# Attention interleaved with an MoE layer: six attention bursts in a group become five, two bursts of group 0 move, and the loads of batches 2 and 3 are asked for later

## Chip, cores and metric

One Trainium2 chip, one core of it. The time is the device time of one execution in microseconds (us). The engines are named as in the profile: PE (TensorE matmul), PEld (its weight loads), DVE (VectorE), ACT (ScalarE), POOL (GpSimd) and SP (SyncE, which here only issues DMAs).

## What is computed

Eight batches of attention (8 heads, 576 positions, 64 dimensions) feed a two-layer MoE block over 8 x 576 = 4608 tokens. The reference, cut to what matters:

```python
q_d, k_d, v_d = (t.reshape(B, H, 144, 4, 64).mean(axis=3) for t in (q, k, v))
out_d     = softmax(q_d @ k_d.T / 8) @ v_d                 # on means of 4 positions
out_up    = np.repeat(out_d, 4, axis=2)
out_local = softmax(where(|i - j| < 4, q @ k.T / 8, -1e9)) @ v
x = (out_up + out_local).transpose(0, 2, 1, 3).reshape(4608, 512)
h = x @ w_in                                               # 512 -> 2048
y = (h / (1 + exp(-1.702 * h))) @ w_out                    # 2048 -> 512
```

## The kernel before

**Groups.** The MoE block runs in nine groups `g` of 512 tokens. `mm1` makes 16 blocks of hidden features (`ffc`), four matmuls of 128x512 each (L706), and ACT turns each block into `gT` (L717). `mm2` multiplies `gT` with `w_out` in 64 matmuls (L771), and `store` evicts each 128 tokens through ACT (`osb`, L756) and asks SP for the output DMA (L761).

**Steps.** The attention of batch `b = g + 1` is cut into steps and laid between the MoE matmuls of group `g` at fixed positions: 0 to 15 are the blocks of `mm1`, and from 16 on one position is one matmul of `mm2`. The order on every engine is the program's order (a manual schedule); engines meet through semaphores that the tile framework sets. The positions are lists:

```python
POS = [13, 16, 33, 44, 55, 65, 74]
POS_0 = [16, 18, 27, 48, 52, 57, 66, 70, 75]
VDP_0 = 44
```

`POS` serves groups 1 to 6 (batches 2 to 7), `POS_0` and `VDP_0` serve group 0 (batch 1). Batch 0 comes ahead of group 0 with code of its own. Groups 7 and 8 hold no attention. A step that puts work on PE is called a burst here. For `POS` the steps are: scores of the first four heads (13), their exponentials on ACT (16, no PE work), scores and exponentials of the other four (33), `avn(0, 1)` (44) and `avn(2, 3)` (55), which multiply the exponentials with the values for two head pairs each, and `tr(0, 1)` (65) and `tr(2, 3)` (74), which turn two head pairs each. That is six bursts. In group 0 the turns come one head pair at a time, and `VDP_0` is one more burst: `prep_vd_pe(1)` (L335) makes the mean values of batch 1 on PE out of `vbs[1]`, which ten DMAs of `load_vb` fill.

**One head pair `hp`.** `av` writes its output to a PSUM tile; `normalise` (DVE: a reciprocal at L477, a product at L478) makes `y`; `transp` (PE: L502 and L487) writes the turned `x` to a PSUM tile; `copy_od` (ACT, two copies, L617) widens the downsampled part into `od`; `merge` (DVE: L638 and a small L644) adds both into `xT[hp]`, the operand of the next group's `mm1`. `xT[hp]` is the hp-th of the four contraction blocks. For groups above 1, `mm1` starts with six matmuls on blocks 0 to 2 and takes block 3 after them.

**PSUM.** Three tiles `PA[0..2]` go round (`ps_tile`), two small ones `PM` serve the MoE blocks. In group 0 the AV outputs and turned tiles use `PA[1]` and `PA[2]` by name.

**Loads.** POOL issues the loads that change the type: `load_qk` (L199; k and q of four heads as bf16, four DMAs for a batch), `load_vb` (L230), `load_w_in`, `load_w_out` (L261). SP issues `load_v` (L219, ten DMAs into the single tile `vf`), `load_v4` (L242, six DMAs) and the stores. In group 0 POOL issues the q/k loads of batch 2 right behind the last `w_out` load, and then a one-element copy (L807) from `w_out` into `vf`, which holds SP's `load_v(2)` until that `w_out` part has landed. In group 1 `load_v(3)` is issued as soon as `prep_v(2)` has read `vf`.

**Preparation in a group.** DVE transposes k and q (`prep_qk`, L276); POOL then, in this order, averages k of the first heads (`pool_qk`, L294 and L297), issues the next batch's q/k loads, casts the values (`prep_v`, L308), averages q, then k and q of the other heads, and last the values (`prep_v4`, L314 and L317). `avn(0, 1)` needs the end of this chain.

Of the kernel before, what the change touches and what calls it, by code (L numbers as in the profile page):

```python
# [8 lines left out]
FP32 = mybir.dt.float32  # L9
# [10 lines left out]
def kernel(  # L20
# [171 lines left out]

    qf, kf, vf = {}, {}, {}

    def load_1(name, src, store, b, qd):
        t = ldp.tile(
            [128, 1152], BF16, name=f"{name}b{qd}", tag=f"{name}b{qd}", bufs=2
        )
        nc.gpsimd.dma_start(  # L199
            out=t,  # L200
            in_=bass.AP(
                tensor=src.tensor, offset=src[b, 4 * qd].offset,
                ap=[[1152, 128], [1, 1152]],
            ),
        )
        store[b, qd] = t

    def load_qk(b, qd):
        load_1("k", k, kf, b, qd)
        load_1("q", q, qf, b, qd)  # L210

    def load_v(b, gate=None, chunks=range(5)):
# [93 lines left out]
    def prep_v(b, eng, i=slice(0, 5), h=slice(0, H)):  # L306
        cp = eng.copy if eng is nc.scalar else eng.tensor_copy
        cp(out=vbs[b % 2][:, i, h, 0:D], in_=vf[b][:, i, h])  # L308
# [14 lines left out]
    def flat(p):  # L323
        return p.rearrange("p x n -> p (x n)")
# [298 lines left out]
    def sub(t, off, *dims):  # L623
        return bass.AP(
            tensor=t.tensor, offset=t.offset + off,
            ap=[list(t.ap[0])] + [list(d) for d in dims],
        )
# [3 lines left out]
    def merge(b, hp, x, od, eng=None):  # L631
        t0 = b * S
        eng = eng or nc.vector
        if eng is nc.gpsimd:
            xs = work.tile([128, 2, 512], BF16, name="xs", tag="xs", bufs=2)
            nc.scalar.copy(out=xs[:, :, 0:288], in_=x[:, :, 0:288])
            x = xs
        eng.tensor_tensor(  # L638
            out=sub(xT[hp], t0 + 3, (57, 2), (114, 5), (1, 57)),
            in0=sub(x, 3, (509, 2), (57, 5), (1, 57)),  # L640
            in1=sub(od, 3, (57, 2), (114, 5), (1, 57)),
            op=ALU.add,
        )
        eng.tensor_tensor(  # L644
            out=sub(xT[hp], t0, (573, 2), (1, 3)),
            in0=sub(x, 0, (512 + 285, 2), (1, 3)),
            in1=sub(od, 0, (573, 2), (1, 3)),
            op=ALU.add,
        )
# [12 lines left out]
    def attention(b, slots=None):  # L662
        st = {}

        def s_pe(qd):
            if qd == 0:
                st["s", qd], st["d", qd] = scores_mixed(b, qd)
            else:
                st["s", qd] = scores(b, qd)
                st["d", qd] = scores_d(b, qd)  # L670

        def s_act(qd):
            if qd == 0:
                nc.scalar.preload_act_table_set("exp_and_others")
            exp_local(qd, st["s", qd])
            exp_down(qd, st["d", qd])
            if qd == 1:
                nc.scalar.preload_act_table_set("silu_and_others")
            mask_local(qd)

        def s1():
            s_pe(1)
            s_act(1)

        def avn(*hps):
            def f():
                ns = [slots and slots[hp % 2] for hp in hps]
                for hp, o in zip(hps, av(b, hps, ns)):
                    st["y", hp] = normalise(o)
            return f  # L690

        def tr(*hps):
            def f():
                ns = [slots and slots[hp % 2] for hp in hps]
                for hp, x in zip(hps, transp(hps, [st["y", hp] for hp in hps], ns)):
                    od = copy_od(hp, x)
                    merge(b, hp, x, od)
            return f

        first = [lambda: s_pe(0), lambda: s_act(0), s1, avn(0, 1)]  # L700
        if b == 1:
            return first + [tr(0), tr(1), avn(2, 3), tr(2), tr(3)]
        return first + [avn(2, 3), tr(0, 1), tr(2, 3)]

    def hps_mm(g, ffc, dmc, acc):
        nc.tensor.matmul(  # L706
# [32 lines left out]
    def mm2(g, gT, steps):  # L739
        tok0 = g * TG  # L740
        n = 0

        if g == 0:
            order = [(t0 + u, 4 * c + f)
                     for t0, c in ((0, 0), (0, 1), (2, 0), (2, 1),
                                   (0, 2), (2, 2), (0, 3), (2, 3))
                     for u in range(2) for f in range(4)]
        else:
            order = [(t, ffc) for t in range(4) for ffc in range(n_ffc)]
        ops = {}  # L750

        def store(t, ap, c0, n, eng, q):
            r0 = tok0 + 128 * t
            osb = moe_sb.tile([128, n], FP32, name="osb", tag=f"osb{n}", bufs=4 if n == 512 else 3)
            if eng is nc.scalar:
                eng.activation(out=osb, in_=ap, func=AF.Copy, scale=1.0 / GELU_SCALE)  # L756
            else:
                eng.tensor_single_scalar(  # L758
                    out=osb, in_=ap, scalar=1.0 / GELU_SCALE, op=ALU.mult
                )  # L760
            q.dma_start(out=out[r0 : r0 + 128, c0 : c0 + n], in_=osb)  # L761

        for t, ffc in order:
            if g == n_groups - 1 and t == 3:
                continue
            for f in steps.get(n, ()):
                f()
            n += 1
            if ffc == 0:
                ops[t] = PA[0][:, t - 2, :] if g == 0 and t > 1 else pm_tile()  # L770
            nc.tensor.matmul(  # L771
                ops[t],
                lhsT=gT[:, ffc, t * 128 : (t + 1) * 128],
                rhs=w_out_bf[:, ffc, :],
                start=(ffc == 0), stop=(ffc == n_ffc - 1),
            )
            if ffc == n_ffc - 1 and not (g == 0 and t == 2):
                for u in (2, 3) if g == 0 and t == 3 else (t,):
                    store(u, ops[u], 0, d_model, nc.scalar, nc.sync)

        if g == n_groups - 1:
            for h in range(2):
                cols = slice(256 * h, 256 * h + 256)
                p = pm_tile()
                for ffc in range(n_ffc):
                    nc.tensor.matmul(  # L786
                        p[:, 0:256],
                        lhsT=gT[:, ffc, 384:512],
                        rhs=w_out_bf[:, ffc, cols],
                        start=(ffc == 0), stop=(ffc == n_ffc - 1),  # L790
                    )
                if h == 0:
                    store(3, p[:, 0:256], 0, 256, nc.scalar, nc.sync)
                else:
                    store(3, p[:, 0:128], 256, 128, nc.scalar, nc.scalar)
                    store(3, p[:, 128:256], 384, 128, nc.vector, nc.sync)
        for f in steps.get(n, ()):
            f()

    POS = [13, 16, 33, 44, 55, 65, 74]  # L800
    POS_0 = [16, 18, 27, 48, 52, 57, 66, 70, 75]
    VDP_0 = 44

    o, y, x = {}, {}, {}

# [93 lines left out]
    for g in range(n_groups):  # L899
        b = g + 1  # L900
        if g == 0:
            nc.gpsimd.memset(v4[32:64], 0.0)
            load_vb(1, 0)
            load_vb(1, 1)
            prep_qk(1, 0)
            pool_qk(1, 0)
            load_vb(1, 2)
            prep_qk(1, 1)
            pool_1(1, 1, "q", nc.vector)
            pool_qk(1, 1, "k")  # L910
            load_vb(1, 3)
            load_vb(1, 4)
            load_w_out(2)
            load_w_out(3)
            for qd in range(NQ):
                load_qk(2, qd)
            load_v(2, gate=after(w_out_bf[0:1, 12, 0:1], nc.gpsimd))
            load_v4(2)
        elif b < B:
            if b > 2:  # L920
                load_v4(b)
            prep_qk(b, 0)
            pool_qk(b, 0, "k")
            if b + 1 < B:
                for qd in range(NQ):
                    load_qk(b + 1, qd)
            prep_v(b, nc.gpsimd)
            if b + 1 < B:
                load_v(b + 1)
            pool_qk(b, 0, "q")  # L930
            prep_qk(b, 1)
            pool_qk(b, 1)
            prep_v4(b, nc.gpsimd)
        steps = {}
        if b < B:
            for n, f in zip(POS if g else POS_0, attention(b, None if g else (1, 2))):
                steps.setdefault(n, []).append(f)
            if g == 0:
                steps.setdefault(VDP_0, []).append(lambda: prep_vd_pe(1, flat(PA[2])))
        gT = new_gT() if g else gT0  # L940
        mm1(g, gT, steps, 0 if g else 6)
        mm2(g, gT, {n - 16: f for n, f in steps.items() if n >= 16})
# [30 lines left out]
```

The softmax here doesn't subtract the row's maximum and nothing guards it: scores larger than these inputs give would overflow.

## Time and profile before

| | |
|---|---|
| runs | 320.34, 324.53, 326.18, 320.25 us |
| median | 322.43 us |
| profiled execution: time, and span in the trace | 320.34 us, 318.6 us |
| PE busy | 311.5 us (98%) |
| ACT, POOL, DVE busy | 183.0, 140.9, 135.3 us |
| granted TensorE clock | 1.000 |
| group 0 from its first step to its end | 38.09 to 60.11 us |
| a group with attention (group 3) | 33.21 us |
| a group without attention (group 7) | 27.72 us |
| DMA moved | 40.02 MB |

The span runs from the first to the last instruction of the program; the time has 1.7 us around it. PE is busy nearly all the time, so a group's length is read from the PE rows, and the other engines matter where PE waits for them. Starts are in us from the beginning of the span. A timeline row gives start, length, engine, line, operation, output and inputs, shapes and count, and in brackets the idle time before it and what ended it.

### The profile page before, as it was taken

The page shows a single profiled execution, that of the slowest core. Times are in us where ns is not written, and L with a number is a line of the kernel's source. Part 1 is how long each engine was busy: PE and PEld are TensorE (multiplying, and loading weights), DVE is VectorE, ACT ScalarE, POOL GpSimd, SP SyncE. Part 2 cuts the span into 40 slices and gives each one's busy share as a digit, 9 for nine tenths or more (in the row PEclk, how much of TensorE's full clock was granted, in tenths as well). Part 3 has the DMA queues.
Part 4 walks back from the last instruction along what each step waited for, and adds up shares of the span by engine and source line. Part 5 has one row for each costly group of instructions (what it writes and reads, how often), then busy time and mean ns, then how long its engine had stood idle before and what let it go on. Part 6 is the DMA issues. An engine that isn't in the chain of part 4 may idle for free.

```text
span 318.6 us, 10869 instructions
## 1 busy us (share of the span) xinstructions
PE 311.5 (98%) x4860; PEld 156.9 (49%) x4860; DVE 135.3 (42%) x224; ACT 183.0 (57%) x317; POOL 140.9 (44%) x172
## 2 busy tenths in 40 slices
PE   7899999999999999999999999999999999999995
PEld 3664554445544555455545544555455544444444
DVE  6983626812674077605670478046811650000000
ACT  4555772667457664668365936593667367315611
POOL 8993960299109930794069604980296000000000
PEclk9999999999999999999999999999999999999999
DMA  7999999899619931994179615981450110020011
GB/s 121 116 196 210 183 140 214 170 200 264 171 61 200 218 96 63 210 207 117 69 165 220 149 70 128 210 194 37 126 92 3 70 68 0 5 95 33 0 67 67
DMA packets 63550, 40.02 MB, mean 126 GB/s; under 512 B 44048, under 2 KB 54416, under 8 KB 63504
## 3 DMA queue, kind: packets, MB, share of 16 engines
q0 software_dynamic: 18864, 14.95, 32.9%
q1 hardware_dynamic: 44496, 24.32, 32.0%
q8 instruction: 38, 0.62, 0.8%
q14 instruction: 8, 0.07, 0.1%
q10 hardware_dynamic: 144, 0.07, 0.1%
HBM read 44.83 MB, written 9.44 MB: 170 GB/s over the span
## 4 chain that ended last, share of the span: by engine, by line
PE 92%; DMA 4%; DVE 1%; POOL 1%; issue 1%; ACT 0%; POOLq 0%; DVEq 0%
PE pm L771 36%; PE pm L706 34%; PE pa L706 6%; PE pa L375 3%; PE pa L771 2%; DMA qb<-in_q_dram 2%; PE pa L394 2%; PE pa L461 2%; PE pa L502 2%; DMA vb<-in_v_dram 1%; PE pa L446 1%; PE pm L786 1%; PE pa L487 1%; DVE y L478 1%; PE pa L590 1%
## 5 line engine op out<-in xcount | busy, mean ns | idle before, releaser
L771 PE MATMUL pm<-w_out_bf,gT 128*128 128x512 bf16 x528 | 121.8, 380 | 0.0
L706 PE MATMUL pm<-xT,w_in_bf 128*128 128x512 bf16 x488 | 109.7, 379 | 0.0
L717 ACT ACTIVATE gT<-pm 128x512 bf16<-128x512 f32 x122 | 72.7, 598 | 38.3 <-PE pm L706 38.2
L706 PEld LDWEIGHTS <-w_in_bf 128*128 128x128 bf16 x576 | 55.6, 98 | 67.1 <-issue 1.9
L771 PEld LDWEIGHTS <-gT 128*128 128x128 bf16 x560 | 51.6, 98 | 59.2 <-issue 0.5
L425 DVE TENSOR_TENSOR es<-es,mask 128x600 bf16<-128x600 bf16 x28 | 20.2, 742 | 82.0 <-ACT es L411 81.6
L294 POOL TENSOR_TENSOR pq<-kT 128x576 f32<-128x576 bf16 x14 | 16.1, 1148 | 85.9 <-DVE kT L276 85.8
L756 ACT ACTIVATE osb<-pm 128x512 f32<-128x512 f32 (+2 forms) x35 | 20.5, 586 | 56.6 <-PE pm L771 52.9
L478 DVE TENSOR_TENSOR y<-pa,rc 128x896 bf16<-128x896 f32 x28 | 30.6, 1091 | 1.0
L638 DVE TENSOR_TENSOR xT<-pa,od 128x570 bf16<-128x570 f32 x28 | 21.1, 753 | 11.8 <-ACT od L617 11.8
L617 ACT COPY od<-pa 128x384 f32<-128x384 f32 (+1 forms) x56 | 18.5, 411 | 12.6 <-DVE xT L644 7.7
L314 POOL TENSOR_TENSOR v<-v 112x512 f32<-112x512 f32 x18 | 24.0, 1331 | 0.0
L758 DVE TENSOR_SCALAR osb<-pm 128x128 f32<-128x128 f32 x1 | 0.3, 292 | 54.8 <-ACT osb L756 54.8
L276 DVE STREAM_TRANSPOSE kT<-kb 128x576 f32<-128x576 f32 x16 | 20.0, 1248 | 3.3 <-DMA kb<-in_k_dram 3.1
L411 ACT ACTIVATE es<-pa 128x600 bf16<-128x600 f32 x32 | 19.7, 667 | 2.7 <-PE pa L375 2.3
L706 PE MATMUL pa<-xT,w_in_bf 128*128 128x512 bf16 x88 | 21.1, 379 | 0.0
L276 DVE STREAM_TRANSPOSE qT<-qb 128x576 f32<-128x576 f32 x16 | 19.9, 1241 | 0.4
L717 ACT ACTIVATE gT<-pa 128x512 bf16<-128x512 f32 x22 | 12.1, 603 | 8.5 <-PE pa L706 8.4
L230 POOL DMA_DIRECT2D vb<-in_v_dram x20 | 13.7, 700 | 6.2 <-DMA w_in_bf<-in_moe_w_in_dram 4.1
L375 PE MATMUL pa<-qT,kT 32*64 32x60 bf16 x1280 | 15.5, 201 | 1.0 <-DVE qT L276 1.0
L375 PEld LDWEIGHTS <-kT 32*64 32x64 bf16 x1280 | 13.8, 103 | 4.5 <-DVE es L425 3.0
L417 ACT ACTIVATE ed<-pa 128x864 bf16<-128x864 f32 x16 | 14.3, 896 | 2.0 <-PE pa L394 1.8
(98 smaller groups left out, 281.2 us busy)
## 6 DMA issues: line engine op xcount, KB each, us to landing
out_dram<-osb SPq DMA_DIRECT2D x35, 256.0 KB, 2.1
vf<-in_v_dram SPq DMA_DIRECT2D x60, 128.0 KB, 4.7
v<-in_v_dram SPq DMA_DIRECT2D x36, 192.0 KB, 5.0
kb<-in_k_dram POOLq DMA_DIRECT2D x16, 288.0 KB, 8.3
qb<-in_q_dram POOLq DMA_DIRECT2D x16, 288.0 KB, 9.4
w_out_bf<-in_moe_w_out_dram POOLq DMA_DIRECT2D x4, 512.0 KB, 8.9
vb<-in_v_dram POOLq DMA_DIRECT2D x20, 64.0 KB, 5.5
w_in_bf<-in_moe_w_in_dram POOLq DMA_DIRECT2D x2, 512.0 KB, 6.2
```

Of the source, the lines that this page charges most:

```text
L276: nc.vector.transpose(out=t32.rearrange("p (i c) -> p c i", c=18), in_=store[b, qd].bitcast(FP32).rearrange("p (c d) -> p c d", c=18),)
L314: eng.tensor_tensor(out=t1[0:112], in0=x[:, :, 0:2, :], in1=x[:, :, 2:4, :], op=ALU.add)
L375: nc.tensor.matmul(sp[r // 2][64 * par : 64 * par + 64, r % 2, 60 * i : 60 * i + 60], lhsT=kT[b, qd][rows, k0 : k0 + 64, a], rhs=qT[b, qd] ...
L411: nc.scalar.activation(out=es[2 * qd + u][:, :, 0:300], in_=sp[u][:, :, 0:300], func=AF.Exp, scale=inv_sqrt_d,)
L425: nc.vector.tensor_tensor(out=ev, in0=ev, in1=mask, op=ALU.mult)
L478: nc.vector.tensor_tensor(out=y[:, xs], in0=ov[:, :, :, 0:D], in1=rc[:, xs].to_broadcast([128, n, 7, D]), op=ALU.mult,)
L617: nc.scalar.copy(out=od[:, 4 * t0 : 4 * (t0 + n)].rearrange("p (t f) -> p t f", f=4), in_=x[:, xx, 288 : 288 + n, None].to_broadcast([128, ...
L638: eng.tensor_tensor(out=sub(xT[hp], t0 + 3, (57, 2), (114, 5), (1, 57)), in0=sub(x, 3, (509, 2), (57, 5), (1, 57)), in1=sub(od, 3, (57, 2) ...
L706: nc.tensor.matmul(acc, lhsT=w_in_bf[:, dmc, ffc * 128 : (ffc + 1) * 128], rhs=xT[dmc][:, g * TG : g * TG + TG], start=(dmc == 0), stop=(d ...
L717: nc.scalar.activation(out=gT[:, ffc, :], in_=acc, func=AF.Silu, scale=GELU_SCALE)
L756: eng.activation(out=osb, in_=ap, func=AF.Copy, scale=1.0 / GELU_SCALE)
L771: nc.tensor.matmul(ops[t], lhsT=gT[:, ffc, t * 128 : (t + 1) * 128], rhs=w_out_bf[:, ffc, :], start=(ffc == 0), stop=(ffc == n_ffc - 1),)
```

## The change

- **Five bursts.** For batches 2 to 7 `avn(2, 3)` and the turn of head pair 0 become one step, `av_and_turn`, at 57; the turns of head pairs 1, 2 and 3 become one step at 70. `merge` of head pair 0 goes from DVE to POOL there: [...]ACT copies the local part of `x` to `xs` in SBUF first. `xs` becomes narrower (288 columns instead of 512) with one buffer.
- **Group 0.** The steps of batch 1 move: the mean values from 44 to 36, `avn(0, 1)` from 48 to 40, the turns of head pairs 0 and 1 from 52 and 57 to 47 and 53, `avn(2, 3)` from 66 to 63. The turns of head pairs 2 and 3 stay at 70 and 75.
- **q and k of batch 2** are no longer asked for ahead of `load_v(2)`. POOL issues them behind the turn of head pair 2, and a one-element copy from `y` of head pair 2 (the third AV output) into the k tile holds them until that `y` is there.
- **v of batch 3** is asked for by SP at position 65 of group 1, behind the store of position 64, instead of behind `prep_v(2)`.
- **Order on POOL.** In groups 1 and 2 POOL averages q of the first heads ahead of `prep_v`.
- The small `osb` tiles get two buffers instead of three.

```diff
-    def load_qk(b, qd):
-        load_1("k", k, kf, b, qd)
+    def load_qk(b, qd, gate=None):
+        load_1("k", k, kf, b, qd, gate)          # load_1 calls gate(t[0:1, 0:1]) ahead of its DMA
         load_1("q", q, qf, b, qd)
...
+        w = 512
         if eng is nc.gpsimd:
-            xs = work.tile([128, 2, 512], BF16, name="xs", tag="xs", bufs=2)
-            nc.scalar.copy(out=xs[:, :, 0:288], in_=x[:, :, 0:288])
-            x = xs
+            xs = work.tile([128, 2, 288], BF16, name="xs", tag="xs", bufs=1)
+            nc.scalar.copy(out=xs, in_=x[:, :, 0:288])
+            x, w = xs, 288
...
         if b == 1:
-            return first + [tr(0), tr(1), avn(2, 3), tr(2), tr(3)]
-        return first + [avn(2, 3), tr(0, 1), tr(2, 3)]
+            def next_qk():
+                tr(2)()
+                load_qk(2, 0, after(st["y", 2][0:1, 0, 0, 0:1], nc.gpsimd))
+                load_qk(2, 1)
+
+            return first + [tr(0), tr(1), avn(2, 3), next_qk, tr(3)]
+
+        def av_and_turn():
+            os = av(b, (2, 3), (None, None))
+            x, = transp([0], [st["y", 0]], [None])
+            for hp, o in zip((2, 3), os):
+                st["y", hp] = normalise(o)
+            merge(b, 0, x, copy_od(0, x), nc.gpsimd)
+
+        return first + [av_and_turn, tr(1, 2, 3)]
...
-            osb = moe_sb.tile([128, n], FP32, name="osb", tag=f"osb{n}", bufs=4 if n == 512 else 3)
+            osb = moe_sb.tile([128, n], FP32, name="osb", tag=f"osb{n}", bufs=4 if n == 512 else 2)
...
-    POS = [13, 16, 33, 44, 55, 65, 74]
-    POS_0 = [16, 18, 27, 48, 52, 57, 66, 70, 75]
-    VDP_0 = 44
+    POS = [13, 16, 33, 44, 57, 70]
+    POS_0 = [16, 18, 27, 40, 47, 53, 63, 70, 75]
+    VDP_0 = 36
...
-            for qd in range(NQ):
-                load_qk(2, qd)
             load_v(2, gate=after(w_out_bf[0:1, 12, 0:1], nc.gpsimd))
...
+            if g < 3:
+                pool_qk(b, 0, "q")
             prep_v(b, nc.gpsimd)
-            if b + 1 < B:
+            if b + 1 < B and g > 1:
                 load_v(b + 1)
-            pool_qk(b, 0, "q")
+            if g > 2:
+                pool_qk(b, 0, "q")
...
+            if g == 1:
+                steps.setdefault(65, []).append(lambda: load_v(3))
```

## The prediction

> **What bounds the kernel now.** I read the page's engine row first, then the busy time of stretches (one group each: its bounds, its length, busy time and instructions of each engine, the granted clock, the DMA share and GB/s), then PE's timeline around each burst.
>
> ```profile
> PE 311.5 (98%) x4860; PEld 156.9 (49%) x4860; DVE 135.3 (42%) x224; ACT 183.0 (57%) x317; POOL 140.9 (44%) x172
> ...
> 60.11:93.56 33.45, 33.45 (x593) 16.61 (x592) 15.60 (x23) 21.41 (x37) 17.76 (x19) 1.00 0.79 177
> ...
> 126.84:160.05 33.21, 33.21 (x594) 16.55 (x592) 16.42 (x25) 20.83 (x36) 17.76 (x19) 1.00 0.65 145
> ...
> 259.77:287.49 27.72, 27.72 (x130) 12.54 (x128) 1.00 (x4) 11.73 (x20) 0.00 (x0) 1.00 0.10 38
> ```
>
> PE fills the span, at a granted clock of 1.00. The last row is group 7, MoE only: 27.72 us; in the chain of waits 64 of its matmuls take 13.81 us, 0.216 each. A group with attention takes 33.21 (group 3), so attention costs 5.5 us of PE time. What the change can win is there, and in group 0. Four bursts of group 2, the same in every later group:
>
> ```profile
> 116.78 2.55 PE L771 MATMUL pm<-w_out_bf,gT 128*128 128x512 bf16 x11
> 119.26 0.29 PE L461 MATMUL pa<-vd,ed 48*64 48x65 bf16 x12
> ...
> 120.00 2.33 PE L771 MATMUL pm<-w_out_bf,gT 128*128 128x512 bf16 x10
> 122.27 0.22 PE L487 MATMUL pa<-id,y 48*64 48x48 bf16 x4
> ...
> 122.80 2.12 PE L771 MATMUL pm<-w_out_bf,gT 128*128 128x512 bf16 x9
> 124.84 0.22 PE L487 MATMUL pa<-id,y 48*64 48x48 bf16 x4
> ...
> 125.38 1.47 PE L771 MATMUL pm<-w_out_bf,gT 128*128 128x512 bf16 x6
> ```
>
> Matmul ends are modelled, so I count starts. Eleven MoE matmuls from 116.78 use up 2.37 us, to 119.15; the MoE is back at 120.00: the AV burst costs **0.85**. Ten from 120.00 end at 122.16, back at 122.80: a turn of two head pairs costs **0.64**; so does the next. Nothing waits inside.
>
> **Five bursts.** Group 0 has turns of one head pair: five MoE matmuls from 50.91 end at 51.99 and the MoE is back at 52.43, 0.44. So a head pair is 0.64 - 0.44 = 0.20, and a burst has a fixed 0.24, for entering and leaving the small tiles. The Trainium skill says the same in kind (TensorEngine Tiling, Key Properties: changing the tiling mode drains the engine); the price is the row's. Now AV 0.85 + turns 0.64 + 0.64 = 2.13. Changed: AV with one turn 0.85 + 0.20 = 1.05, three turns 0.64 + 0.20 = 0.84, together 1.89. Saved 0.24 a group, in six groups **-1.4**. No row has AV and turns in one burst. Bounds: 0 (a switch inside after all) and -1.4; the AV burst mixes 48- and 64-row matmuls at no visible cost, and turns are 48 and 60 rows, so I take -1.4.
>
> Does anything become late? A is the first AV matmul of the step at 57; the MoE resumes at A + 0.95 and the turns start after 13 matmuls (2.81) and an entry of 0.10, at **A + 3.86**.
>
> - y of pair 3: in the row at 85.84 DVE ends it at 89.16, A + 3.32. Margin 0.5.
> - x of pair 0 must leave PSUM before x of pair 3 takes its tile: ACT od 0.66 and xs about 0.65 (es of 600 columns takes 0.67), done by A + 2.4. Cover 1.5 us.
> - xT of pair 3, T being the first turn of the burst of three: od pairs 0.66 each from T + 0.5, the third waiting for the first merge (two od buffers), and merges 0.87 apart on DVE end at T + 3.95. PE wants it after 0.73 of burst, 10 matmuls, and the six of blocks 0 to 2: T + 4.18. Margin 0.2; before it was as thin (merge ends 94.63, PE at 94.68, no gap).
> - xT of pairs 1 and 2 are done at T + 2.2 and T + 3.1, wanted at T + 3.1 and T + 3.3.
>
> **The merge on POOL** is where a rule speaks against the change. One add, the same shape, on both engines:
>
> ```profile
> L294 POOL TENSOR_TENSOR pq<-kT x14: 1142/1147/1167, 31.5 to 234.8; 128x576 f32<-128x576 bf16 x14
> ...
> L294 DVE TENSOR_TENSOR pq<-qT x3: 742/746/771, 10.6 to 35.0; 128x576 f32<-128x576 bf16 x3
> ```
>
> The row makes POOL 1.54 times slower: merge 0.75 x 1.54 = 1.16, with the small add about 1.4. The skill (GPSIMD Engine Reference, Engine selection) says VectorE should do it, POOL being about 2 times slower: 1.5, with the small add 1.8. From A + 2.4 that ends at A + 3.8 or A + 4.2; xT of pair 0 is wanted at position 80, A + 0.95 + 23 matmuls + 0.73 = A + 6.6, and od's buffer at A + 5.0. Neither price reaches the end: cost 0. POOL's next work waits for kT of the next group and sat idle 15.35 us there. L425, with two SBUF inputs, has gone from 457 to 1542 ns on DVE, the long ones while POOL worked; y reads PSUM and stayed at 1090 to 1093, but never beside a POOL add. A rival takes this up.
>
> **Group 0.**
>
> ```profile
> 49.22 1.04 PE L771 MATMUL pm<-w_out_bf,gT 128*128 128x512 bf16 x4
> 50.58 0.35 PE L502 MATMUL pa<-id,y 60*64 60x60 bf16 x20 [0.32 <-DVE y L478]
> ...
> 55.22 1.04 PE L771 MATMUL pm<-w_out_bf,gT 128*128 128x512 bf16 x4
> 56.51 0.34 PE L502 MATMUL pa<-id,y 60*64 60x60 bf16 x17 [0.26 <-DVE y L478]
> 57.13 0.22 PE L502 MATMUL pa<-id,y 60*64 60x57 bf16 x3 [0.28 <-issue]
> ...
> 57.33 0.60 PE L771 MATMUL pm<-w_out_bf,gT 128*128 128x512 bf16 x2
> ```
>
> Here PE waits for DVE: four matmuls after AV are too few. The turn of pair 0 costs 50.08 to 50.91 = 0.83 where 0.44 is normal, that of pair 2 costs 56.08 to 57.33 = 1.25. With seven matmuls between, y (ready 2.0 us after AV's start) comes 0.3 us before its turn. Saved 0.39 + 0.81 = **-1.2**. Of this 0.49 is the "issue" gap at 57.13, with no wait behind it; the other three turns have none, so I count it as gone, and -0.7 is the other bound.
>
> The burst at 36 starts 9 matmuls after 42.81, at 44.85. The last load of vb was issued at 40.62 and lands 4.4 us later, 45.05; its chunk is read by the last two of 14 matmuls, at 45.45. Margin 0.4; below that the burst waits one for one. ACT's cast behind it finds its table load ending at 45.84, when PE is done: no delay. AV four matmuls later has its values as just in time as before (48.41 for 48.47). PSUM tiles, `w_out` (landed 51.0, wanted about 54) and the end of the group (turn at 75, as before) stay in order.
>
> **q and k of batch 2.** With y of pair 2 at 55.4 and the gate copy (0.18, as L807) POOL issues k at 55.65 instead of 42.80. What depends on it:
>
> ```profile
> 61.95 1.14 POOL L294 TENSOR_TENSOR pq<-kT 128x576 f32<-128x576 bf16 x1 [10.72 <-DVE kT L276]
> ...
> 79.68 0.84 POOL L317 TENSOR_TENSOR vd<-v 112x256 bf16<-112x256 f32 x1
> ```
>
> From kT to vd POOL has no gap: 18.6 us, and AV of group 1, at 82.61 and now 1.2 sooner at 81.4, wants vd. With the transpose (1.25) and semaphores k must land by **61.4**. Scores at 13 are easier, q being pooled ahead of the 2.3 us cast: k by 62.8. How long does the load take? The quickest k took 4.6 us from issue, on an empty queue. The one in group 1, issued at 63.78, took 8.4, because six v4 loads stood before it; hardly any of its packets moved until they were through. The skill (DMA: Bandwidth & Descriptors, Queues, rings and completion order) says the engines go round between queues packet by packet; then SP's loads would share with k rather than go first. By that rule k lands at about 59; by the row it stands behind what SP has issued. With q/k gone, `load_v(2)` moves from 51.26 on its own, ten issues 0.67 apart against about 0.65 of transfer each, so hardly anything is queued at 55.65: k lands near 59.5, q at 61.4, v4 by 72 as before. I take 59.5, cost 0; bounds 59 and 64.1 (8.4 us).
>
> **The rest.** The ten issues of `load_v(3)` leave SP's queue at 68.6 to 82.5 and stand behind the store of position 64, from about 87.2; the next store and `load_v4(3)` wait behind them, about 1 us later than before. vf lands by about 97, wanted by `prep_v(3)` at about 100. The small osb buffers cost nothing.
>
> **Sum.** 318.6 - 1.4 - 1.2 = 316.0 of span; the profiled execution's 320.34 becomes **317.7**. The four runs shown go from 320.25 to 326.18 with a median of 322.43, from which the same 2.6 gives 319.8. I name the middle, **318.8**. A measurement tells about 2% from no change; this is 0.8%.
>
> **Rivals.**
>
> 1. *No joint saving*: AV and turn switch inside the burst. Group 0 alone remains: 319.1 on the profiled scale. Against it: nothing between 48, 60 and 64 rows shows.
> 2. *k is late by the row of 8.4 us*: landed 64.1, AV of group 1 waits 2.7: 320.4, no difference. For it: the page's median of 8.3 for k. Against it: those had v4 before them.
> 3. *Slower*: k and q go behind all of `load_v(2)` and `load_v4(2)`. The queue empties near 72, four loads of 1.4 us go last, k lands at 67.8, and POOL's chain ends 6.4 us too late for AV: 324.1. It decides from 61.4 on, one for one. For it: in group 1 k stood behind all v4. Against: here most v4 are issued after k.
> 4. *DVE and POOL collide*: y of pair 3 grows by up to 1.0, as L425 did; with 0.5 of margin, 0.5 x 6 = 3: 320.7. Against it: y starts at A + 2.23, before the add.
>
> **Chances.** Forecast 0.60, rival 1 0.10, rival 2 0.12, rival 3 0.08, rival 4 0.06, something unseen 0.04. Range 316.5 to 323.5: below, every run on the profiled scale with a little more gained; above, rivals 2 to 4 on the scale of the median. Over 2% faster (under 316.0) has no mechanism, 0.05; over 2% slower needs rival 3 and more, 0.05.
>
> **What would show it.** Right: groups 2 to 6 at 33.0; bursts of 1.05 and 0.84; no DVE release before L502 in group 0, which ends near 58.9; AV of group 1 after 11 matmuls without a gap; k landing before 61.4. Wrong: a PE wait on POOL or DVE at scores or AV of group 1, on L335 at 44.9, or on y or xT at the step at 70 and the first block-3 matmuls.

## The result: the same in the ratio, with about half of the runs several us longer

The changed kernel took 324.25 us (median of 35 runs, 319.59 to 329.88), the kernel before 321.07 us (56 runs, 319.99 to 326.18; the four shown before are among them). The ratio after to before is **1.0002, interval 0.998 to 1.0025**. The ratio leaves out runs more than 1.5% above the fastest of their own kernel, 15 of the changed kernel's; that is why a median 1% higher stands beside it. Of the changed kernel's 36 runs 19 lie above 323 us, and in a second session 9 of 22; of the kernel before 28 of 260 over all sessions. So two questions are open: where the forecast gain of 2.6 us went in the undisturbed runs, and what makes the others long.

The profiled execution took 322.58 us, its span 320.8. Its first group step begins at 41.84 us, 3.8 later than before, because PE ran at half clock for 6.8 us from 21.7 on, ahead of every step that the change moves. From the first step to the end it needs 278.97 us, before 280.54: **1.6 us less**. The busy time of stretches, group 0 from its first step and groups 1 to 3 (bounds, length, busy time and instructions of PE, PEld, DVE, ACT and POOL, granted clock, DMA share, GB/s):

```profile
41.84:62.56 20.72, 20.72 (x544) 11.08 (x544) 10.02 (x19) 11.90 (x20) 4.24 (x9) 1.00 0.87 137
62.56:96.24 33.68, 33.34 (x594) 16.77 (x593) 16.98 (x22) 22.07 (x38) 19.55 (x21) 1.00 0.67 163
96.24:129.53 33.29, 33.26 (x593) 16.76 (x592) 16.84 (x23) 21.42 (x38) 19.42 (x21) 1.00 0.81 176
129.53:162.64 33.11, 33.11 (x593) 16.67 (x592) 15.32 (x23) 21.48 (x38) 19.21 (x21) 1.00 0.69 146
```

Group 0 of the kernel before, counted in the same way from the first matmul of its first step to the first of group 1 (the table before has other bounds, 38.09 and 60.11):

```profile
38.02:59.94 21.92, 21.07 (x543) 11.17 (x543) 9.97 (x20) 11.89 (x20) 7.06 (x12) 1.00 1.49 174
```

So group 0 is 1.2 us shorter than before. Group 3 is 0.10 shorter (33.21). But group 1 is 0.23 *longer* (33.45) and group 2 as long as it was (33.28): there something ate the gain of the five bursts. PE's timeline of the changed kernel in group 1 shows it, and in group 2 the two new bursts:

```profile
82.75 2.55 PE L786 MATMUL pm<-w_out_bf,gT 128*128 128x512 bf16 x11
85.22 0.26 PE L463 MATMUL pa<-vd,ed 48*64 48x65 bf16 x8
85.82 0.23 PE L463 MATMUL pa<-vd,ed 48*64 48x65 bf16 x4 [0.34 <-POOL vd L319]
...
86.50 1.68 PE L786 MATMUL pm<-w_out_bf,gT 128*128 128x512 bf16 x7
...
119.80 2.98 PE L786 MATMUL pm<-w_out_bf,gT 128*128 128x512 bf16 x13
122.70 0.29 PE L463 MATMUL pa<-vd,ed 48*64 48x65 bf16 x12
...
123.34 0.37 PE L504 MATMUL pa<-id,y 60*64 60x60 bf16 x20
123.52 0.23 PE L489 MATMUL pa<-id,y 48*64 48x48 bf16 x6
123.68 2.98 PE L786 MATMUL pm<-w_out_bf,gT 128*128 128x512 bf16 x13
126.59 0.24 PE L489 MATMUL pa<-id,y 48*64 48x48 bf16 x6
...
127.36 2.33 PE L786 MATMUL pm<-w_out_bf,gT 128*128 128x512 bf16 x10
```

Read as in the prediction: 13 MoE matmuls from 119.80 use 2.81, to 122.61; the MoE is back at 123.68, so AV with one turn costs **1.07**. Thirteen from 123.68 end at 126.49, back at 127.36: three turns cost **0.87**. The first burst, `avn(0, 1)` of group 1, costs 85.12 to 86.50 = **1.37** where 0.84 is normal, and the row names the cause: PE waits for the mean values that POOL makes last. POOL's timeline of the same kernel, with the chain behind it, the merge, and the cast of batch 3's values:

```profile
59.30 0.18 POOL L822 COPY kb<-y 1x1 bf16<-1x1 bf16 x1 [7.20 <-DVE y L480]
59.81 0.56 POOL L201 DMA_DIRECT2D kb<-in_k_dram  x1 [0.33 <-POOL kb L822]
...
66.85 1.14 POOL L296 TENSOR_TENSOR pq<-kT 128x576 f32<-128x576 bf16 x1 [4.89 <-DVE kT L278]
...
84.94 0.83 POOL L319 TENSOR_TENSOR vd<-v 112x256 bf16<-112x256 f32 x1
91.87 1.24 POOL L641 TENSOR_TENSOR xT<-xs,od 128x570 bf16<-128x570 bf16 x1 [6.10 <-ACT xs L639]
...
105.95 2.32 POOL L310 CAST vb<-vf 128x2560 bf16<-128x2560 f32 x1 [1.51 <-DMA out_dram<-osb]
```

The chain of 18.9 us from L296 to L319 runs with one pause of 0.26, but starts at 66.85 because k was asked for late. The cast at 105.95 waited 1.51 us. The release is put down to a store, but the store has nothing that this cast reads: the last of the ten loads into `vf` landed at 105.90.

Two suspects follow, one for each moved load.

### The profile page after: what moved, and what is told of

Same layout as the page of the kernel before. It is cut to its first block, busy times and chain, and to the rows that moved or that the text cites. A ratio compares the mean times of both kernels' runs of the same rounds, so it can differ in the third digit from the quotient of the medians.

```text
span 320.8 us, 10881 instructions
## 1 busy us (share of the span) xinstructions
PE 313.1 (98%) x4860; PEld 158.2 (49%) x4860; DVE 133.1 (41%) x212; ACT 186.9 (58%) x323; POOL 150.4 (47%) x185
## 4 chain that ended last, share of the span: by engine, by line
PE 72%; POOL 11%; DMA 10%; issue 5%; DVE 1%; ACT 0%; POOLq 0%; DVEq 0%
PE pm L786 32%; PE pm L721 27%; DMA qb<-in_q_dram 7%; PE pa L721 4%; DMA w_out_bf<-in_moe_w_out_dram 3%; PE pa L377 2%; POOL pq L296 2%; POOL vb L232 2%; PE pa L463 2%; PE pa L396 1%; POOL kb L201 1%; POOL v L316 1%; PE pa L504 1%; PE pa L448 1%; PE pm L801 1%
## 5 line engine op out<-in xcount | busy, mean ns | idle before, releaser
L786 PE MATMUL pm<-w_out_bf,gT 128*128 128x512 bf16 x528 | 120.4, 380 | 0.0
L427 DVE TENSOR_TENSOR es<-es,mask 128x600 bf16<-128x600 bf16 x28 | 22.2, 810 | 81.4 <-ACT es L413 80.9
L296 POOL TENSOR_TENSOR pq<-kT 128x576 f32<-128x576 bf16 x14 | 16.1, 1147 | 30.6 <-DVE kT L278 30.5
L641 POOL TENSOR_TENSOR xT<-xs,od 128x570 bf16<-128x570 bf16 x6 | 7.4, 1240 | 47.3 <-ACT xs L639 47.3
L641 DVE TENSOR_TENSOR xT<-pa,od 128x570 bf16<-128x570 f32 x22 | 16.6, 754 | 12.8 <-ACT od L619 12.8
```

The lines of the kernel that those rows point to most:

```text
L296: eng.tensor_tensor(out=t1, in0=sv[:, :, 0:2, :], in1=sv[:, :, 2:4, :], op=ALU.add)
L427: nc.vector.tensor_tensor(out=ev, in0=ev, in1=mask, op=ALU.mult)
L641: eng.tensor_tensor(out=sub(xT[hp], t0 + 3, (57, 2), (114, 5), (1, 57)), in0=sub(x, 3, (w - 3, 2), (57, 5), (1, 57)), in1=sub(od, 3, (57, ...
L786: nc.tensor.matmul(ops[t], lhsT=gT[:, ffc, t * 128 : (t + 1) * 128], rhs=w_out_bf[:, ffc, :], start=(ffc == 0), stop=(ffc == n_ffc - 1),)
```

## Experiments

The first four runs were made to tell late loads (A in their expectations) from a longer start (B). What came out of them is the theory that the later runs test.

**Theory.** v of batch 3 comes late (V, where an expectation uses the letter): behind the store of position 64 its last load runs into the q/k loads of batch 4, `prep_v(3)` waits, and PE waits for it in group 2. Rivals: q/k of batch 2 are late and cost the gain in group 1; the five bursts or group 0 gain nothing in themselves; the long runs come from the chip and not from the kernel.

All runs follow. The kernel before had medians of 320.79 us beside e1 to e4, 321.06 beside f1 to f4 and 320.94 beside h1 to h4.

| kernel | median us (runs) | ratio to before, interval | runs above 323 us |
|---|---|---|---|
| changed | 324.25 (35) | 1.0002, 0.998 to 1.0025 | 19 of 36 |
| e1: changed, again | 321.44 (22) | 0.9986, 0.9966 to 1.0007 | 9 of 22 |
| e2: q/k of batch 2 early | 325.55 (22) | 1.0026, 0.9991 to 1.0061 | 18 of 22 |
| e3: v of batch 3 early | 319.96 (22) | 0.9972, 0.995 to 0.9994 | 1 of 22 |
| e4: both early | 320.38 (22) | 0.998, 0.9966 to 0.9993 | 0 of 22 |
| f1: v of batch 3 at 34 | 320.36 (22) | 0.9971, 0.9944 to 0.9998 | 4 of 22 |
| f2: q/k of batch 4 behind v | 319.97 (22) | 0.9962, 0.9938 to 0.9986 | 3 of 22 |
| f3: five bursts alone | 320.42 (22) | 0.9979, 0.9956 to 1.0001 | 0 of 22 |
| f4: group 0 alone | 321.54 (22) | 1.0004, 0.9979 to 1.0029 | 3 of 22 |
| h1: q/k of batches 3 and 4 later | 319.14 (22) | **0.9947, 0.9929 to 0.9966** | 0 of 22 |
| h2: q/k of batch 2 alone | 324.09 (6) | **1.0094, 1.0071 to 1.0117** | 5 of 6 |
| h3: v of batch 3 alone | 320.86 (22) | 1.0018, 1.0 to 1.0036 | 3 of 22 |
| h4: as h1, old group 0 | 320.14 (17) | 0.9989, 0.997 to 1.0009 | 2 of 17 |

### e1 to e4: which of the moved loads

e1 is the changed kernel once more.

> The changed kernel once more, for a second profile and as the measure for the three below. In its first profile group 0 onward took 1.6 us less than before (my sum said 2.6), while the stretch ahead of group 0's first step was 3.8 us longer with a half clock for 6.8 us. Theory A (late loads): on an undisturbed start PE is earlier against the loads, so AV of group 1, which waited 0.5 us there, waits 1.5 to 2 us and eats the gain: ratio about 1.00, the AV burst of group 1 at 2.3 to 2.9 us instead of 0.85. Theory B (start only): the groups keep their 1.6 us and the start alone is longer: AV of group 1 stays at 1.4 or below and a start like that of the kernel before gives a ratio of 0.995.

Measured: 0.9986, 9 of 22 above 323. Both kinds of run are there again, in another proportion. AV of group 1 cost 0.88, so the wait of theory A did not come; nor did the 0.995 of theory B. From its first step to the end this profile, with an undisturbed start, needs 280.44 us: 0.1 less than before, where the first profile had 1.6 less.

e2 asks for q/k of batch 2 at the old place:

```diff
-                load_qk(2, 0, after(st["y", 2][0:1, 0, 0, 0:1], nc.gpsimd))
-                load_qk(2, 1)
...
+            for qd in range(NQ):
+                load_qk(2, qd)
             load_v(2, gate=after(w_out_bf[0:1, 12, 0:1], nc.gpsimd))
```

> The changed kernel with one part undone: q and k of batch 2 are asked for where they were before, ahead of load_v(2). Theory A: no wait at AV of group 1, which costs 0.85 again; 1.5 to 2 us faster than the changed kernel, ratio to before about 0.993. Theory B: same time as the changed kernel within 0.5 us. Rival C (the old place is bad for the values: v of batch 2 lands later and AV waits for it): no gain either, AV of group 1 still waits.

Measured: AV of group 1 went back to 0.84, so that wait was q/k's. But the kernel as a whole got no faster (1.0026), and 18 of 22 runs were long. Its profile is one of the long ones, and shows the mechanism in full. POOL's timeline in group 2:

```profile
97.22 0.57 POOL L201 DMA_DIRECT2D kb<-in_k_dram  x1
...
100.65 0.66 POOL L299 TENSOR_TENSOR qdT<-pq 128x288 bf16<-128x288 f32 x1
107.94 2.32 POOL L310 CAST vb<-vf 128x2560 bf16<-128x2560 f32 x1 [6.62 <-DMA out_dram<-osb]
```

PE's timeline of the same run:

```profile
114.85 2.55 PE L784 MATMUL pm<-w_out_bf,gT 128*128 128x512 bf16 x11
...
118.73 0.23 PE L463 MATMUL pa<-vd,ed 48*64 48x65 bf16 x4 [1.17 <-POOL vd L319]
120.75 0.27 PE L463 MATMUL pa<-vd,ed 48*64 48x65 bf16 x4 [1.79 <-POOL vd L319]
...
121.83 3.90 PE L784 MATMUL pm<-w_out_bf,gT 128*128 128x512 bf16 x13
```

The cast waits 6.62 us, everything behind it on POOL is late, the second scores of group 2 cost 2.98 us (normal 1.32) and AV(0, 1) 4.59 (normal 0.84). Then the 13 MoE matmuls from 121.83 take 3.90 us instead of 2.98. The stretch says why; the clock is the figure before the DMA share:

```profile
120.30:123.70 3.40, 2.95 (x73) 1.75 (x73) 2.13 (x4) 0.00 (x0) 0.39 (x1) 0.50 0.02 5
```

PE had stood almost idle from 117.4 to 120.75, and from 120.3 on it was granted half clock for 3.4 us. From first step to end this run needs 285.87 us, 6.9 more than the profile of the changed kernel.

Why the cast waited is in the DMA view of e2. The queues (kind: packets, MB, share of 16 engines), first from 98 to 99 us, then from 103 to 107:

```profile
q1 hardware_dynamic: 692, 0.17, 76.2%
q0 software_dynamic: 3, 0.01, 18.3%
```

```profile
q0 software_dynamic: 306, 0.63, 82.8%
q1 hardware_dynamic: 308, 0.31, 27.6%
```

q1 is SP's queue with v, q0 POOL's with the four q/k loads of batch 4. Until 99 the loads into `vf` have the engines to themselves and move 692 packets in 1 us, of 0.17 MB / 692 = 250 bytes. From 103 on q0 moves 306 packets in 4 us, 2 KB each, and q1 as many. Only 109 of q1's are `vf`'s, of 256 bytes, 27 in 1 us; most of the others belong to the store and the `load_v4` that stand behind it on the same queue. Packet for packet both queues get about the same, so the load with the small packets starves. The last `vf` load, asked for at 97.45, landed at 107.88, the q/k loads at 102.72 to 108.59. That the engines go round between queues is what the Trainium skill states (DMA: Bandwidth & Descriptors, Queues, rings and completion order). The share isn't always one to one: beside q/k of batch 2 in h1 (62 to 66 us) q1 had 934 packets to 310.

e3 leaves q/k late and asks for v of batch 3 at the old place:

```diff
-            if b + 1 < B and g > 1:
+            if b + 1 < B:
                 load_v(b + 1)
...
-            if g == 1:
-                steps.setdefault(65, []).append(lambda: load_v(3))
```

> The changed kernel with the other load undone: v of batch 3 is asked for behind prep_v(2) in group 1, as before. In the first profile prep_v(3) waited 1.5 us for it in group 2 and AV there cost 1.09 instead of 0.85. Theory A and B alike: 0.25 us from group 2. If the transfers of v then stand before q and k of batch 3, another group may wait instead: no gain.

Measured: 0.9972, one run above 323. AV of group 2 costs 0.84 and its `prep_v(3)` starts at 101.62 without a wait. In group 1 the wait of AV for POOL stays (burst of 1.92).

e4 makes both of these edits.

> Both load moves undone: five bursts, the positions of group 0 and the order on POOL remain. Theory A: my whole sum appears, 2.6 us less than before, ratio 0.992. Theory B: 0.5 us less than the changed kernel at most, ratio 0.998 or more.

Measured: 0.998, the figure of theory B and not the 0.992 of A, and no run above 323; AV of groups 1 and 2 at 0.87 and 0.84. So v of batch 3 makes the long runs, and q/k of batch 2 cost nothing that the ratio shows (e3 against e4), although AV of group 1 waits for them.

### f1 to f4: the same cause from the other side, and the two other parts alone

f1 asks for v of batch 3 at position 34 of group 1, behind another store:

```diff
-                steps.setdefault(65, []).append(lambda: load_v(3))
+                steps.setdefault(34, []).append(lambda: load_v(3))
```

> The changed kernel with one position altered: v of batch 3 is asked for at 34 of group 1 instead of 65. In the changed kernel its last transfer, issued at 96.5, landed at 102.6 in one run; with q and k of batch 2 early it was issued at 97.5 and landed at 107.9, 10 us later, behind q and k of batch 4 (issued from 97.2), and prep_v(3) and AV of group 2 waited 5 us. Theory V (the tail of v of batch 3 is caught behind q and k of batch 4): 31 matmuls and two bursts sooner it lands well before 97; AV of group 2 costs 0.85; hardly a run over 323 us (the changed kernel had 28 of 58 there), median about 320.0, ratio about 0.997. Theory S (the start of the kernel makes these runs long): still about half the runs over 323.

f2 keeps v of batch 3 at 65 and takes away what it collides with: in group 2 POOL issues the q/k loads of batch 4 behind `prep_v(3)`, not ahead of it.

```diff
-            if b + 1 < B:
+            if b + 1 < B and g != 2:
                 for qd in range(NQ):
                     load_qk(b + 1, qd)
...
             prep_v(b, nc.gpsimd)
+            if g == 2:
+                for qd in range(NQ):
+                    load_qk(b + 1, qd)
```

> The changed kernel with v of batch 3 left at 65, but POOL issues q and k of batch 4 in group 2 behind prep_v(3) instead of ahead of it. Theory V: nothing can stand beside the tail of v of batch 3; it lands about 3 us after its issue, near 99.5; prep_v(3) waits for nothing (it is due at about 99), few runs over 323, ratio about 0.997. If instead the late issue at 65 alone is the cause (theory I), the waits at AV of group 2 and the long runs stay.

Measured: f1 0.9971, f2 0.9962. In f1 the last `vf` load is issued at 88.08 and lands at 91.86, long before q/k of batch 4. In f2 it is issued at 96.50 as late as in e1, lands at 100.10 instead of 102.62, and AV of group 2 is undisturbed. (`prep_v(3)` still waited 1.34 us, where no wait was expected: without the four issues ahead of it, it is due 2.3 us sooner.) It is the collision that costs, not the position 65 itself. Long runs fell to 4 and 3 of 22, beside 12 of 75 of the kernel before in that session.

f3 is the kernel before with the five bursts (and the merge on POOL and the smaller buffers), f4 the kernel before with the new `POS_0` and `VDP_0`.

```diff
f3
-        return first + [avn(2, 3), tr(0, 1), tr(2, 3)]
+        return first + [av_and_turn, tr(1, 2, 3)]
...
-    POS = [13, 16, 33, 44, 55, 65, 74]
+    POS = [13, 16, 33, 44, 57, 70]
f4
-    POS_0 = [16, 18, 27, 48, 52, 57, 66, 70, 75]
-    VDP_0 = 44
+    POS_0 = [16, 18, 27, 40, 47, 53, 63, 70, 75]
+    VDP_0 = 36
```

> The kernel before with the five bursts alone (av_and_turn at 57, three turns at 70, merge of pair 0 on POOL); group 0, loads and POOL order as before. By my sum -1.4 us; by the bursts of the changed kernel's profile (1.07 + 0.87 against 0.84 + 0.63 + 0.63) -0.16 a group, -1.0 us: ratio 0.997. If merging is worth nothing on the chip: 1.000. If the turn of three makes xT late: over 1.000 with a gap at the first block-3 matmuls.

> The kernel before with the positions of group 0 alone. By my sum -1.2 us, of which 0.49 was a gap without a wait at the turn of pair 2. If that gap belongs to a fixed place in PE's instruction stream (it has stood at the same matmul, the 992nd, in three of six profiles, and another at the 864th in two), it stays or comes back elsewhere: -0.7, ratio 0.998. If it went with the wait: 0.996.

Measured: the five bursts alone 0.9979, 0.7 us (0 to 1.4). Group 0 alone 1.0004, between 0.7 gained and 0.9 lost. In f4's trace the two DVE waits are gone, as forecast; the "issue" gap is not. It stands ahead of the same three matmuls as before. Rows of PE's timeline, first of f4, then of f3:

```profile
56.64 0.22 PE L502 MATMUL pa<-id,y 60*64 60x57 bf16 x3 [0.53 <-issue]
```

```profile
58.28 0.22 PE L502 MATMUL pa<-id,y 60*64 60x57 bf16 x3 [1.23 <-issue]
```

### h1 to h4: a better version, and the late loads by themselves

h1 carries f2 on: in group 1 POOL issues the q/k loads of batch 3 behind `prep_v4(2)`, in group 2 those of batch 4 behind `prep_v(3)`. All the rest is the changed kernel.

```diff
-            if b + 1 < B:
+            if b + 1 < B and g > 2:
                 for qd in range(NQ):
                     load_qk(b + 1, qd)
...
             prep_v(b, nc.gpsimd)
+            if g == 2:
+                for qd in range(NQ):
+                    load_qk(b + 1, qd)
...
             prep_v4(b, nc.gpsimd)
+            if g == 1:
+                for qd in range(NQ):
+                    load_qk(b + 1, qd)
```

> The changed kernel with two POOL orders altered: q and k of batch 3 are asked for behind prep_v4(2) in group 1, q and k of batch 4 behind prep_v(3) in group 2. If AV of group 1 waits because k of batch 2 lands late (62.1 to 62.4 instead of the 61.4 at which my sum put the edge) and POOL's chain behind it is 18.6 us, then taking the 2.4 us of DMA issues out of that chain ends the wait: AV of group 1 at 0.85 (it cost 0.9 to 1.9 with late q/k), and with group 2 mended as well a ratio of about 0.995, no gap at the 992nd matmul. If AV of group 1 waits for something else (v4, the mask on DVE), it still costs over 1.2.

Measured: 319.14 us, **0.9947 (0.9929 to 0.9966)**, none of 22 above 323: faster than both kernels. The ratio is the one expected, but the route is not, so the number is in part luck. AV of group 1 was to come back to 0.85 and costs 1.48 in the profile. Two rows of POOL's timeline, `prep_v(2)` and `prep_v(3)`:

```profile
69.41 2.32 POOL L310 CAST vb<-vf 128x2560 bf16<-128x2560 f32 x1 [2.24 <-DMA v<-in_v_dram]
...
100.78 2.32 POOL L310 CAST vb<-vf 128x2560 bf16<-128x2560 f32 x1 [2.09 <-DMA out_dram<-osb]
```

The 2.2 us that the four issues no longer take on POOL turned into a wait for v of batch 2. Its last load was issued at 59.03 and landed at 69.29, 10.3 us later, beside q/k of batch 2: the same collision one batch earlier. In group 2 a wait of 2.09 for a late v is left, but it ends at 100.78 instead of 107.94.

h2 and h3 put one late load each on the kernel before: h2 `next_qk` with its gate, h3 the `load_v(3)` at 65.

> The kernel before with q and k of batch 2 moved behind the third AV output, alone. Theory L: k lands near 63, POOL's chain ends near 82.9 and AV of group 1 (82.6 before) waits 0 to 1 us; against it, the gap at the 992nd matmul of PE (0.4 to 1.4 us in all five kernels with q/k early, none in five with q/k late) goes: -0.5 or more. Together within 0.5 us of before, ratio 0.998 to 1.001. If the gap stays, it isn't the loads that make it.

Measured: 1.0094, 3.0 us slower. The expectation missed in the time. (One part came true: with nothing but the q/k loads moved, the gap behind the 991st matmul is gone; the last section comes back to it.) h2 has the old order on POOL, q averaged behind the cast. POOL's timeline, then PE's:

```profile
68.96 2.32 POOL L310 CAST vb<-vf 128x2560 bf16<-128x2560 f32 x1 [0.98 <-DMA v<-in_v_dram]
71.26 1.14 POOL L296 TENSOR_TENSOR pq<-qT 128x576 f32<-128x576 bf16 x1
72.47 0.67 POOL L299 TENSOR_TENSOR qdT<-pq 128x288 bf16<-128x288 f32 x1
```

```profile
73.19 0.26 PE L396 MATMUL pa<-qdT,kdT 32*64 32x144 bf16 x4 [2.20 <-POOL qdT L299]
...
74.50 4.04 PE L713 MATMUL pm<-xT,w_in_bf 128*128 128x512 bf16 x12
```

The scores at 13 wait 2.20 us for q, and the 12 MoE matmuls behind them take 4.04 us where the same 12 take 2.76 in group 2 of the changed kernel: half clock for 3.4 us from 73.7. In the changed kernel q's average stands ahead of the 2.3 us cast and of its wait for v. That part of the change, which the prediction used in half a sentence, is what makes the late q/k affordable; that it does so alone was not run, it follows from the rows.

> The kernel before with v of batch 3 asked for at 65 of group 1, alone; POOL casts it ahead of averaging q, so it is due about 1.8 us sooner than in the changed kernel. Theory V: its last transfer is caught behind q and k of batch 4, prep_v(3) and AV of group 2 wait, and most runs are over 323 us: median about 325, ratio of the runs kept 1.005 or more. If the five bursts or group 0 are needed for the long runs: as before.

Measured: 1.0018, 3 of 22 above 323. The theory as it stood at that point, that position 65 makes the long runs, missed too. The order of issues explains it:

| | last `vf` load issued | first q/k of batch 4 issued | `vf` landed | `prep_v(3)` waited |
|---|---|---|---|---|
| h3 | 96.28 | 97.32 | 99.37 | 0 |
| e1 | 96.52 | 97.06 | 102.62 | 1.53 |
| changed | 99.90 | 100.35 | 105.90 | 1.51 |
| e2 | 97.45 | 97.22 | 107.88 | 6.62 |
| f2 | 96.50 | 102.42 | 100.10 | 1.34 |
| h1 | 97.59 | 103.04 | 100.72 | 2.09 |

(us; the starts of the changed kernel are 3 to 4 later throughout.) A lead of 1.04 us over the q/k loads lets the last `vf` load land in 3.1 us; with 0.5 it takes 6.0, with none 10.4. In h3, where group 1 still has its six bursts, the lead is just enough; the changed kernel stands on the edge, and which side a run falls on is a matter of half a microsecond of SP's and POOL's timing. That fits that one kernel has both kinds of run; only one profile of each kernel is there, so the link from a long run to this wait is shown in full for e2 alone. The granted clock of each run speaks for it too. One half-clock stretch of 3.4 us gives a run a mean clock of 0.995 (profiles of e2 and h2), 6.8 us give 0.989 (profile of the changed kernel). A clock of 0.993 to 0.995 stands in 29 of the 80 runs of the changed kernel, e1 and e2, and in 28 of their 46 long ones; in 1 of 44 of e3 and e4, none of 22 of h1 and 2 of 204 of the kernel before (beside the experiments), whose 18 long runs have 0.989 or less in 16 cases. So most long runs of the changed kernel hold one such stretch, as after a late v, and most of those before are of another kind. Some long runs have another origin: the kernel before has them too (28 of 260), and the profiled execution of the changed kernel lost its time at the start.

h4 is h1 with the old `POS_0` and `VDP_0`; "the first" in its expectation is h1.

> As the first of this call, but group 0 with its old positions. Alone on the kernel before the new positions gave 1.0004. If they are worth my 0.7 us where q and k of batch 2 are late: ratio 0.997, 0.7 us above the first of this call. If nothing: the same as it.

Measured: 0.9989, against 0.9947 for h1, which is 1.3 us, and alone (f4) the new positions were worth nothing that can be seen. But the two profiles don't put the 1.3 us into group 0, which takes 21.44 us in h4 and 21.19 in h1. The rest lies in group 1, 35.06 against 33.75, where the two programs are the same. PE's timeline of h4 there:

```profile
88.52 0.34 PE L504 MATMUL pa<-id,y 60*64 60x60 bf16 x19 [1.78 <-issue]
```

PE stood still for 1.8 us, in the middle of the turn, with no wait for another engine. So these profiles show 0.25 us for the new group 0; how much of the 1.3 is owed to such gaps is open.

## Why the prediction missed

The median of 324.25 us lies above the whole range that was named (up to 323.5), because about half of the runs are long. The step that failed is the one on v of batch 3, under "The rest"; the others are smaller.

- **Five bursts: right in kind, 0.08 too much a group.** 1.07 + 0.87 = 1.94 for 1.05 + 0.84 = 1.89; with 0.84 + 0.63 + 0.63 = 2.10 read from the trace before, 0.16 a group is saved and 1.0 in six, not 0.24 and 1.4. The term that was mis-sized is the head pair added to a burst: 0.23 and 0.24 where 0.20 was put. Rival 1, no joint saving, is out by these bursts, which cost the same in all undisturbed groups; f3, the bursts alone, measured 0.7 with an interval down to 0.
- **The merge on POOL: right.** 1.24 + 0.20 us, close to the estimate of 1.4 from the row and under the 1.8 from the factor of 2; nothing waited for it, and no wait on `y` or `xT` appeared at the step at 70 or in the first block-3 matmuls (rival 4 out).
- **Group 0: the two DVE waits went, the 0.49 did not go reliably.** All four turns cost 0.43 in the profile after. The "issue" gap in the turn of pair 2 is absent there, in e1, e3, f1, f2 and h1, but stands in e2, e4, f3 and f4 (and in the kernel before), all with q/k of batch 2 early; h3, early too, has none. In its place e1 and h1 have one in the turn of pair 1: 0.78 and 0.17. "I count it as gone" was the wrong choice of the two bounds. The values' burst at 36 cost 1.01 in the profile after; e1 shows 1.26, so the margin of 0.4 against the last `vb` load was thin. In e3 PE waits 0.28 us at 50.20 for the third of the four `w_out` loads, where the prediction looked at the last alone. In all, group 0 takes 20.7 to 22.1 us with the new positions (the changed kernel, e1 to e4, h1) and 21.4 with the old ones where the gap happens to be absent (h2, h3, h4): the 1.2 us of the first profile are its best case, with the gap of the kernel before in its favour.
- **q and k of batch 2: a miss of size.** k was issued 0.5 to 1.3 us later than worked out (the 0.33 behind the gate copy, for one, was left out) and landed 5.1 to 5.9 us after issue, not 3.85, in e1, e3 and h1 at 62.0 to 62.4: past the edge of 61.4, within the bounds. AV of group 1 paid 0.53 in the profile after, 0 to 1.4 in the others. The prediction weighed the rule of turns by packet only for what it does to k. In the rows above it came out at about one to one in e2 and at three to one in h1, and what it does above all is slow the *small* packets, those of v behind k: the last `vf` load of batch 2 landed 9 to 10 us after its issue (e1, h1), and `prep_v(2)` waited for it in h1, h2, h4 and f1.
- **"The rest": the step that failed.** v of batch 3, priced at nothing with "lands by about 97, wanted about 100". Issues were counted rightly, but they left SP from 89.9 to 96.5 (e1) where the prediction had 87.2 and ten issues of 0.67, and the q/k loads of batch 4, which the prediction named nowhere here, go out at 97. The tail landed at 102.6 to 107.9, and with v late 28 of 58 runs were long (changed, e1), against 1 of 44 with v early (e3, e4). No rival held this: the third had q/k behind v, and what happened was v behind q/k, one batch on.
- **The scale.** The 2.6 us were set between the profiled execution and the median of four runs, 322.43; over 56 runs the median before is 321.07, so 318.8 stood 2.3 below it and not 3.6.

Sum over the groups in the profile after: -1.2 in group 0, +0.23 and +0.01 in groups 1 and 2, -0.10 to -0.17 in each of the four others: -1.6. In e1's profile, the same kernel, it is -0.1: +0.13 in group 0, +0.23 in group 2, and +0.20 in group 4, where an "issue" gap of 0.28 stands. The ratio of 1.0002 fits that on average the gaps and the late v take back what the bursts give; no run separates the two. The parts together, without the late loads, give 0.998 (e4), and the change with its collisions moved, 0.9947 (h1). Why h1 beats e4, when its profile is 0.5 us longer from the first step on (279.60 against 279.12) and its start 0.8 shorter, stays open.

## What to carry to other kernels

When a load is asked for later, list every transfer in flight beside it by packet size, on all queues: a load in 250-byte packets that meets one in 2 KB packets loses most of its rate, and its tail can land with the other's, even when it was asked for first. A load moved to the edge may pay nothing in most runs and several microseconds in the rest, so look at the spread of the runs and not at the ratio alone. Parts of a change can carry one another (here POOL's order and the late q/k), so a part that is worth nothing or harmful alone isn't therefore idle in the whole.

## What was not expected of the hardware

- **A wait of PE is paid twice.** In h2 a single wait of 2.20 us, in e2 a stretch of 3.4 us with two short pieces of work in it, was followed by 3.4 us at clock 0.50. The 1.78 us gap in h4 was not. The Trainium skill (TensorE: Matmul & The Clock Gate, Part 1) speaks of an idle window of about 3.4 us; here a wait of 2.2 was enough, and in the 3.4 us ahead of the half clock PE was busy for 1.20 (h2, 70.3 to 73.7).
- **PE stops at fixed places of its program.** The "issue" gaps lie behind matmul 223 and 351 (the changed kernel, ahead of group 0), 863 (e1, e2, h1), 991 (before, e2, e4), 1502 (h4) and 3163 (e1, e2). The distances are multiples of 128 matmuls within four; a matmul with its weight load is two instructions. The page of the changed kernel has a queue that fits:

```profile
q8 instruction: 38, 0.62, 0.9%
```

38 packets, 16 KB each; PE has 9720 instructions, 38 times 256. The traces hold the time of each of these packets. In the ten that have all 4860 matmuls, every gap of 0.15 us or more ends 1.3 to 1.5 us after the end of the packet of its turn (the seventh for matmul 991), and at none of the 37 places in any of them does PE go on sooner than 1.28 us after it. So the gaps are waits for the next block of 256 instructions. What holds the packet up is shown for matmul 991: h2 differs from the kernel before in the q/k loads of batch 2 alone. The seventh packet in the DMA view of the kernel before from 54.6 to 55.6 us, then of h2 from 51.5 to 54.5:

```profile
q8 instruction: 1, 0.02, 6.2%
```

```profile
q8 instruction: 1, 0.02, 3.0%
```

It starts at 54.61 us before and at 51.82 in h2, and the gap is gone. With these loads early (before, e2, e4, f3, f4, h3) it starts at 54.1 to 55.8, with them late (e1, e3, f1, f2, h1, h2, h4) at 51.5 to 53.0; h3, early without a gap, reaches the place 1.35 us after the packet, just in time. By which step the loads hold it up is open.
